# Partial sums of an output product added in DRAM by DMAs that GpSimd issues, instead of on VectorE

## The chip, the cores and the metric

The kernel runs on one core of one Trainium2 chip. The metric is the device time of one execution in microseconds (us); lower is better. TensorE is written PE (its weight loads PEld), VectorE DVE, ScalarE ACT, GpSimd POOL and SyncE SP, as in the profile.

## The reference, cut to what matters

Causal attention over 2 batches of 12 heads (448 positions, 64 wide) gives a matrix x of 896 tokens by 768 features. Two dense stages follow.

```python
a = x @ w1;  b = x @ w2
y = (a * b @ w3) @ w_out                 # first stage, 768 -> 1024 -> 768
h = y @ w_in                             # second stage, 768 -> 2048
g = h * clip(h + 3.0, 0.0, 6.0) / 6.0
out = g @ moe2_w_out                     # 2048 -> 768
```

The last product is the one the change touches. The kernel calls its weights v_out and it works on transposed data: the result is 768 rows (6 blocks of 128) by 896 columns (2 halves of 448).

## The kernel before, in words

Every 32-bit product is made of three passes: each operand is split into a high and a low part, and high*high, high*low and low*high are accumulated in one PSUM bank. A matmul here is 128 by 128 weights against 448 columns. Some products use a seven-product scheme of Strassen's kind (P1 to P7), in which sums and differences of blocks are formed by DVE ahead of time.

The 2048 rows of the last product are cut into NC = 4 parts of 512, c = 0 to 3, so that a part can be multiplied as soon as its piece of g is there. The list `work` gives the order: `pg` units (`gated`, line 943) make g, `po` units (`collected`, line 1049, for c = 0, 1, 2, and `joined`, line 1012, for c = 3) multiply it by v_out. For c = 1, 2, 3 the order is pg, po, pg, po, po, each po belonging to the part before; the three `joined` units come last, each of them with the seven products on banks X, Y and Z.

A `collected(c, i)` unit has four groups of 12 matmuls, for row blocks m = i and i + 3 (j = 0, 1) and halves b = 0, 1. Each group fills one bank, and `evict` (line 772) empties it. The sums of the parts live in DRAM, in `sums_of[m, b]`, 128 by 448 words (224 KB) each. For c = 0, ACT copies the bank to an SBUF tile `o` and SP stores it. For c = 1 and 2, SP first loads the old sum into `o`, DVE adds the bank to it, and SP stores `o` again. `joined` loads the sums of three parts into four tiles `o[m, b]`, adds its seven products to them on DVE and stores to `out`.

The tiles `o` come from tags with two buffers each: `c22` for b = 0, `a2` for b = 1. The tag `a2` also carries a value of `gated`, the tags `a1` and `r` serve `joined(1)`. In the order of the program the last users of `a2` are: `gated(7)`, groups 2 and 4 of `collected(2, 1)`, groups 2 and 4 of `collected(2, 2)`, then `o[0, 1]` and `o[1, 1]` of `joined(0)`. A tile can be filled only when the user two places before it is done with the buffer.

What is issued on each engine, and in what order, is fixed when the kernel is built, by a list scheduler (`Plan.issue`). It goes through the operations in simulated time; each engine takes the ready operation of the lowest rank. Ranks in this part are `DENSE` plus the unit's number; a unit's weights are prepared two units ahead (`ahead`, rank + `AHEAD`). The planner's costs are written in the code: an SP issue 0.6 us and 3.2 us more until the data is there (line 94), a copy of a bank on ACT 0.06 + 448 * 0.00083 us, an addition on DVE 0.065 + 448 * 0.00104 us, a result of PE 0.2 us after its end, others 0.15 us. An operation on POOL counts as landed 0.1 us after its end, and lasts longer by every DVE operation marked `ports` that starts beside it (lines 203 to 212); the splits of weights are so marked. On the chip each engine then runs its list in that order and waits on semaphores.

POOL's own work in this part is splitting weights (line 337, tiles vja, vjb for pg, voa for `joined`).

Of the kernel before, what the change touches and what calls it, by code (L numbers as in the profile page):

```python
# [14 lines left out]
ALU = mybir.AluOpType  # L15
# [19 lines left out]
DENSE = 100.0  # L35
# [182 lines left out]
def attention_moe_moe2(ctx: ExitStack, tc, q, k, v, w1, w2, w3, w_out, v_in, v_out, out):  # L218
# [8 lines left out]
    nc = tc.nc  # L227
    B, H, S, D = SHAPE
# [69 lines left out]
    def act(n, sb=False):  # L298
        return n * 0.00105 if sb else 0.06 + n * 0.00083

    def dve(n):
        return 0.065 + n * 0.00104
# [157 lines left out]
    plan = Plan()  # L460
# [9 lines left out]
    def scratch(tag, name):  # L470
        if tag == "a1":
            return plan.tile(lambda: xp.tile([P, S], F32, tag=tag, name=name, bufs=2), tag, 2)
        return plan.tile(lambda: later["ab"].tile([P, S], F32, tag=tag, name=name, bufs=2), tag, 2, (done2,))
# [232 lines left out]
    for p in range(HK):  # L706
        x, b, b11, b21 = xt[p, 1], bf[p + HK], xt[p, 0], xt[p + HK, 0]
# [21 lines left out]
    def dense_bank(name):  # L729
        return plan.tile(lambda: later["ps"].tile([P, 512], F32, tag="dl", name=name), "psdl", 8 - DENSE_BANKS, (done,))  # L730

    def bank(name):
        i = count["bank"] % 8
        count["bank"] += 1
        if i < DENSE_BANKS:
            return plan.tile(lambda: pd.tile([P, 512], F32, tag="d", name=name), "psd", DENSE_BANKS)
        return dense_bank(name)

    def cols(b):
        return slice(b * S, (b + 1) * S)  # L740

    def halves(t, b):
        return [t.at((b, HI)), t.at((b, LO))]
# [27 lines left out]

    def evict(ps, m, b, n, c, o):
        rank = DENSE + n
        if c:
            plan.op("dve", dve(S), lambda: nc.vector.tensor_tensor(o[:, :], ps[:, :S], o[:, :], ALU.add),  # L775
                    reads=[ps], writes=[o], rank=rank)
        else:
            plan.op("act", act(S), lambda: nc.scalar.copy(o[:, :], ps[:, :S]), reads=[ps], writes=[o], rank=rank)
        plan.op("sp", 0.6, lambda: nc.sync.dma_start(sums_of[m, b], o[:, :]),
                reads=[o], writes=[summed.at((m, b))], rank=rank)  # L780


    ab, open_ = {}, {}
# [35 lines left out]
    def spare(name):  # L819
        return plan.tile(lambda: later["t"].tile([P, S], F32, tag="c22", name=name, bufs=2), "c22", 2, (done,))  # L820
# [61 lines left out]
    n = after_jobs  # L882
# [38 lines left out]
    for p in range(HK):  # L921
        group = [(m, b) for b in range(B) for m in (p, p + HK)]
        ps = {g: bank("px%d_%d" % g) for g in group}
        for kk in range(KF):
            for m, b in group:
                def go(kk=kk, m=m, b=b, n=n + (m != p), ps=ps):
                    for a, c in ((HI, HI), (HI, LO), (LO, HI)):
# [5 lines left out]
                        writes=[ps[m, b]], rank=DENSE + n)  # L933
# [5 lines left out]
    sums_of = dp.tile([KD, B, P, S], F32, name="sums_of")  # L939
    summed = Handle(plan, None, None, 0)  # L940
# [108 lines left out]
    def collected(c, i):  # L1049
        n = first_of["po", c, i]  # L1050
        for j in range(2):
            m = i + HK * j
            for b in range(B):
                name = f"po{c}_{m}_{b}"
                ps = dense_bank(name) if j else plan.tile(
                    lambda name=name: pd.tile([P, 512], F32, tag="d", name=name), "psd", DENSE_BANKS)
                o = scratch("a2", f"o{c}_{m}_{b}") if b else spare(f"o{c}_{m}_{b}")
                if c:
                    plan.op("sp", 0.6, lambda o=o, m=m, b=b: nc.sync.dma_start(o[:, :], sums_of[m, b]),
                            reads=[summed.at((m, b))], writes=[o], rank=DENSE + n - 2)  # L1060
                for kk in range(KC):
                    def go(ps=ps, n=n, at_=((j * 2 + kk % 2) * 2 + kk // 2) * P, k=c * KC + kk, kk=kk, b=b):
                        for a, d in ((HI, HI), (HI, LO), (LO, HI)):
                            nc.tensor.matmul(  # L1064
                                ps[:, :S], hls[n][:, a, at_:at_ + P], gt[k][:, d, cols(b)],
                                start=kk == 0 and a == d, stop=kk == KC - 1 and a == LO)

                    plan.op("pe", 0.6, go, kind="r", reads=[hls[n], *halves(gt[c * KC + kk], b)], writes=[ps], rank=DENSE + n)
                evict(ps, m, b, n, c, o)

    for w in work:
        if w[0] == "pg":
            gated(w[1])
            for i in range(2):
                ahead(first_of[w] + i)
        else:
            joined(w[2]) if w[1] == NC - 1 else collected(*w[1:])
            ahead(first_of[w])
            while pending:
                between(*pending.pop())  # L1080
# [66 lines left out]
```

## Time and profile before

| | us |
|---|---|
| median of 3 runs | 543.11 (542.46 to 543.97) |
| the profiled execution | 543.72 |
| its span, first to last instruction | 541.9 |
| PE busy in the span | 533.7 |
| DVE / ACT / POOL busy | 407.5 / 306.3 / 120.6 |

The profile is of one execution. The span leaves out some 1.8 us around the instructions. The part that the change touches runs from about 405 us (the first `pg` unit after c = 0) to 512 us, and `joined` runs from there to the end.

### The profile page before, as it was taken

What the parts mean: (1) busy time and instruction counts of PE and PEld (TensorE: products, weight loads), DVE (VectorE), ACT (ScalarE), POOL (GpSimd) and SP (SyncE); (2) the same over time, 40 slices, a digit from 0 to 9 for tenths busy, and PEclk for the clock granted to TensorE, in tenths of its full rate; (3) what the DMA queues carried; (4) which work ended last, traced back from release to release, by engine and by line L of the source; (5) the groups of instructions that cost most, each with busy time, mean ns of one, the idle gap of its engine ahead of it and who ended that gap; (6) DMA issues with size and microseconds to landing.
All of it is one profiled execution on the core that took longest, in us unless ns stands there. A gap on an engine that the chain in (4) does not pass through costs nothing.

```text
span 541.9 us, 8054 instructions
## 1 busy us (share of the span) xinstructions
PE 533.7 (98%) x2863; PEld 482.6 (89%) x2863; DVE 407.5 (75%) x778; ACT 306.3 (57%) x597; POOL 120.6 (22%) x156
## 2 busy tenths in 40 slices
PE   8999999999999999999999999999999999999997
PEld 6787887789999999999999998899899999999996
DVE  4998887647914799897728649999947795799664
ACT  4987878877425555544525335978655651666100
POOL 4787874540501111120000111000000000010100
PEclk9999999999999999999999999999999999999999
DMA  8988876214133333322513012628283857372745
GB/s 289 356 291 268 320 245 206 91 62 158 47 114 131 117 116 117 118 97 99 212 60 116 1 59 76 236 97 317 79 285 110 269 183 259 112 252 76 256 152 186
DMA packets 33512, 89.91 MB, mean 166 GB/s; under 512 B 3264, under 2 KB 21952, under 8 KB 30912
## 3 DMA queue, kind: packets, MB, share of 16 engines
q1 hardware_dynamic: 33472, 89.40, 48.4%
q8 instruction: 22, 0.36, 0.3%
q14 instruction: 18, 0.15, 0.1%
HBM read 75.24 MB, written 14.16 MB: 165 GB/s over the span
## 4 chain that ended last, share of the span: by engine, by line
PE 88%; DVE 5%; issue 3%; DMA 1%; ACT 1%; POOL 0%; SPq 0%; POOLq 0%; DVEq 0%
PE po L1064 15%; PE pw L664 12%; PE paX L812 11%; PE px L928 10%; PE pgX L812 8%; PE s L529 7%; PE paZ L812 5%; PE o L595 4%; PE pgZ L812 4%; PE ptp L578 4%; PE paY L812 3%; PE pgY L812 2%; PE poX L812 1%; PE warm L621 1%; DMA ks<-in_k 1%
## 5 line engine op out<-in xcount | busy, mean ns | idle before, releaser
L1064 PE MATMUL po<-g,vo 128*128 128x448 f32 x432 | 87.9, 362 | 0.0
L1064 PEld LDWEIGHTS po<-g,vo 128*128 128x128 f32 x432 | 81.0, 187 | 5.4
L664 PE MATMUL pw<-wr,w 128*128 128x384 f32 x384 | 69.9, 340 | 0.0
L664 PEld LDWEIGHTS pw<-wr,w 128*128 128x128 f32 x384 | 66.4, 188 | 0.5
L555 POOL TENSOR_SCALAR prb<-prb,sums 128x64 f32<-128x64 f32 (+6 forms) x84 | 58.7, 715 | 36.0 <-DVE sums L549 24.5
L928 PE MATMUL px<-ab,wp 128*128 128x448 f32 x288 | 57.8, 362 | 0.0
L928 PEld LDWEIGHTS px<-ab,wp 128*128 128x128 f32 x288 | 54.0, 187 | 3.6
L536 ACT ACTIVATE prb<-prb,sums 128x64 f32<-128x64 f32 (+6 forms) x84 | 42.1, 505 | 12.9 <-DVE sums L532 12.4
L529 PE MATMUL s<-ks,qs 128*128 128x128 f32 (+6 forms) x168 | 46.1, 399 | 1.4 <-DMA ks<-in_k 1.2
L337 POOL TENSOR_SCALAR vja<-vir 128x768 fp32r<-128x768 f32 x8 | 7.7, 957 | 172.2 <-DVE x2t L751 70.1
L532 DVE CUSTOM_DVE_ANT_0 prb<-s,maskb 128x64 f32<-128x64 f32 (+6 forms) x84 | 32.8, 415 | 14.1 <-PE s L529 11.9
L529 PEld LDWEIGHTS s<-ks,qs 128*128 128x128 f32 x168 | 26.9, 195 | 8.0 <-DVE sums L532 2.9
L583 ACT COPY pt<-ptp 128x512 f32<-128x512 f32 x48 | 26.2, 584 | 9.2 <-PE ptp L578 9.1
L578 PE MATMUL ptp<-ident,prb 128*128 128x128 f32 x192 | 27.0, 273 | 0.0
L337 POOL TENSOR_SCALAR w2a<-w1r 128x768 fp32r<-128x768 f32 x8 | 14.4, 1799 | 55.2 <-PE paZ L812 37.2
L578 PEld LDWEIGHTS ptp<-ident,prb 128*128 128x128 f32 x192 | 22.5, 141 | 4.2 <-issue 1.7
L595 PEld LDWEIGHTS o<-pt,vr 128*64 128x64 f32 x192 | 12.7, 136 | 13.0 <-issue 8.7
L595 PE MATMUL o<-pt,vr 128*64 128x448 f32 (+3 forms) x192 | 23.4, 386 | 0.0
L756 ACT ACTIVATE rab<-q,consts 128x448 f32<-128x448 f32 x24 | 16.1, 673 | 12.3 <-DVE q L956 12.3
L775 DVE TENSOR_TENSOR o<-po,o 128x448 f32<-128x448 f32 x24 | 14.9, 620 | 9.9 <-PE po L1064 6.9
L361 ACT ACTIVATE vor<-vor 128x1024 f32<-128x1024 f32 x12 | 13.9, 1161 | 14.5 <-DMA vor<-in_moe_w_out 14.5
L766 ACT ACTIVATE g<-rab 128x448 fp32r<-128x448 f32 x28 | 16.5, 589 | 6.3 <-DVE rab L759 5.6
(181 smaller groups left out, 1157.5 us busy)
## 6 DMA issues: line engine op xcount, KB each, us to landing
vor<-in_moe_w_out SPq DMA_DIRECT2D x12, 1024.0 KB, 5.3
w3r<-in_moe_w SPq DMA_DIRECT2D x8, 1024.0 KB, 7.2
sums_of<-o SPq DMA_DIRECT2D x36, 224.0 KB, 3.2
o<-sums_of SPq DMA_DIRECT2D x36, 224.0 KB, 2.9
wrr<-in_moe_w_out SPq DMA_DIRECT2D x8, 768.0 KB, 7.5
w1r<-in_moe_w SPq DMA_DIRECT2D x8, 768.0 KB, 5.7
w2r<-in_moe_w SPq DMA_DIRECT2D x8, 768.0 KB, 4.3
vjr<-in_moe_w_in SPq DMA_DIRECT2D x8, 768.0 KB, 4.8
```

What stands on the lines that cost most here:

```text
L337: plan.op("pool", single(size), lambda: nc.gpsimd.tensor_scalar(hl[:, HI, at_:at_ + size], x(), 1.0, 1.0, ALU.mult, ALU.mult), reads=reads ...
L529: plan.op("pe", pe4(n), lambda: nc.tensor.matmul(ps[:, :n], qs[u][:, t].rearrange("p h i -> p (h i)"), ks[u][:, :n], start=True, stop=True ...
L532: plan.op("dve", dve(n), lambda: nc.vector.tensor_tensor_reduce(out=z(), in0=ps[:, :n], in1=maskb[:, S - n:], scale=-SCALE, scalar=3.0e38, ...
L536: plan.op("act", 0.29 + n * 0.00083, lambda: nc.scalar.activation(z(), z(), AF.Exp, bias=sm[:, 0, t:t + 1], scale=-1.0, accum_out=sm[:, 1, ...
L555: nc.gpsimd.tensor_scalar(s, s, sm[:, 1, t:t + 1], 1.0, ALU.mult, ALU.mult)
L578: nc.tensor.transpose(ps[:, i * P:(i + 1) * P], pb[:, OFF[t] + kb * P:OFF[t] + (kb + 1) * P], ident)
L583: plan.op("act", act(4 * P), lambda: nc.scalar.copy(d[:, 4 * g:4 * g + 4].rearrange("p n h i -> p (n h i)"), ps[:, :]), reads=[ps], writes ...
L595: nc.tensor.matmul(ps[T * j:T * j + T, kb * P:S], vr[u][:, kb, j, :], d[:, base[kb]:base[kb] + TQ - 2 * kb, j, :], start=kb == 0, stop=kb ...
L664: nc.tensor.matmul(ps[:, :W], weight(n, a, kk), hls[m][:, c, at_:at_ + W], start=kk == 0 and a == c, stop=kk == KF - 1 and a == LO)
L812: nc.tensor.matmul(ps[:, :S], hl[:, a, off + kk * P:off + (kk + 1) * P], t[:, c, at_], start=first and kk == 0 and a == c, stop=kk == n - ...
L928: nc.tensor.matmul(ps[m, b][:, :S], weight(n, a, kk), ab[kk][:, c, cols(b)], start=kk == 0 and a == c, stop=kk == KF - 1 and a == LO)
L1064: nc.tensor.matmul(ps[:, :S], hls[n][:, a, at_:at_ + P], gt[k][:, d, cols(b)], start=kk == 0 and a == d, stop=kk == KC - 1 and a == LO)
```

## The change

For c = 1 and 2, ACT copies the bank to `o` as it does for c = 0, with no load ahead of it. Then POOL issues a DMA that adds `o` to `sums_of[m, b]` in DRAM. The 24 loads by SP (12 per part), the 24 additions on DVE and the 24 stores by SP go; 24 copies on ACT and 24 adding DMAs on POOL's queue come. `joined` is as it was, with its 12 loads of the sums. The planner counts the adding DMA as a POOL operation of 1.0 us.

```diff
     def evict(ps, m, b, n, c, o):
         rank = DENSE + n
+        plan.op("act", act(S), lambda: nc.scalar.copy(o[:, :], ps[:, :S]), reads=[ps], writes=[o], rank=rank)
         if c:
-            plan.op("dve", dve(S), lambda: nc.vector.tensor_tensor(o[:, :], ps[:, :S], o[:, :], ALU.add),
-                    reads=[ps], writes=[o], rank=rank)
+            plan.op("pool", 1.0, lambda: nc.gpsimd.dma_start(sums_of[m, b], o[:, :], accum_op=ALU.add),
+                    reads=[o], writes=[summed.at((m, b))], rank=rank)
         else:
-            plan.op("act", act(S), lambda: nc.scalar.copy(o[:, :], ps[:, :S]), reads=[ps], writes=[o], rank=rank)
-        plan.op("sp", 0.6, lambda: nc.sync.dma_start(sums_of[m, b], o[:, :]),
-                reads=[o], writes=[summed.at((m, b))], rank=rank)
+            plan.op("sp", 0.6, lambda: nc.sync.dma_start(sums_of[m, b], o[:, :]),
+                    reads=[o], writes=[summed.at((m, b))], rank=rank)
@@ collected
                 o = scratch("a2", f"o{c}_{m}_{b}") if b else spare(f"o{c}_{m}_{b}")
-                if c:
-                    plan.op("sp", 0.6, lambda o=o, m=m, b=b: nc.sync.dma_start(o[:, :], sums_of[m, b]),
-                            reads=[summed.at((m, b))], writes=[o], rank=DENSE + n - 2)
                 for kk in range(KC):
```

## Rows read from the trace of the kernel before

**Rows 1.** The page: the span, and busy time of each engine (share, instructions).

```profile
span 541.9 us, 8054 instructions
PE 533.7 (98%) x2863; PEld 482.6 (89%) x2863; DVE 407.5 (75%) x778; ACT 306.3 (57%) x597; POOL 120.6 (22%) x156
```

**Rows 2.** Windows A:B: length, busy us of PE, PEld, DVE, ACT, POOL; clock; DMA.

```profile
361.40:404.40 43.00, 41.86 (x210) 38.75 (x209) 34.83 (x51) 29.35 (x47) 1.94 (x2) 1.00 0.57 196
404.40:458.40 54.00, 54.00 (x272) 50.63 (x271) 41.28 (x63) 27.79 (x42) 3.93 (x4) 1.00 0.64 211
458.40:512.40 54.00, 54.00 (x271) 50.44 (x270) 45.39 (x78) 26.80 (x43) 5.85 (x6) 1.00 0.52 170
```

**Rows 3.** Timeline of PE: start us, us, line, tiles, count, idle before.

```profile
383.23 2.08 PE L812 MATMUL pgX<-T4g,v 128*128 128x448 f32 x9 [1.14 <-DVE q L956]
...
458.35 1.96 PE L812 MATMUL pgX<-x2t,vja 128*128 128x448 f32 x9
...
512.46 1.36 PE L812 MATMUL poX<-g,voa 128*128 128x448 f32 x6
...
514.87 1.42 PE L812 MATMUL poX<-T2o,voc 128*128 128x448 f32 x6
516.12 1.36 PE L812 MATMUL poZ<-T1o,voa 128*128 128x448 f32 x6
517.32 1.36 PE L812 MATMUL poX<-g,voa 128*128 128x448 f32 x6
...
522.12 1.36 PE L812 MATMUL poZ<-T1o,voa 128*128 128x448 f32 x6
523.56 0.88 PE L812 MATMUL poX<-T3o,voa 128*128 128x448 f32 x3
...
536.88 1.36 PE L812 MATMUL poX<-g,voc 128*128 128x448 f32 x6
```

**Rows 4.** The chain that ended last, its end: start us, us, what.

```profile
536.53 1.76 DMA out<-o
538.29 0.61 DVE o L1027
```

**Rows 5.** One line's instructions, L775 and then L778: ns min/median/max, first and last start.

```profile
L775 DVE TENSOR_TENSOR o<-po,o x24: 609/622/626, 420.0 to 514.7; 128x448 f32<-128x448 f32 x24
...
L778 ACT COPY o<-po x12: 512/534/581, 365.7 to 404.6; 128x448 f32<-128x448 f32 x12
```

**Rows 6.** The stores L779, then the loads L1059: issue ns, and issue to landing.

```profile
L779 SPq DMA_DIRECT2D sums_of<-o x36: 319/319/382, 366.3 to 515.3; - x36
...
DMA to landing us min/median/max: 1.9/3.2/7.5
...
L1059 SPq DMA_DIRECT2D o<-sums_of x24: 319/320/481, 403.2 to 510.2; - x24
...
DMA to landing us min/median/max: 2.4/2.7/5.4
```

**Rows 7.** Timeline of SP's queue at the handover to `joined`.

```profile
515.30 0.32 SPq L779 DMA_DIRECT2D sums_of<-o  x1
...
517.75 1.90 SPq L1023 DMA_DIRECT2D o<-sums_of  x3
```

**Rows 8.** Timeline of DVE at the handover.

```profile
513.12 1.10 DVE L343 TENSOR_TENSOR voc<-vor,voc 128x256 fp32r<-128x256 f32 x3 [1.24 <-ACT voc L341]
...
514.66 0.61 DVE L775 TENSOR_TENSOR o<-po,o 128x448 f32<-128x448 f32 x1
...
523.43 1.14 DVE L1027 TENSOR_TENSOR o<-poZ,o 128x448 f32<-128x448 f32 x2
```

**Rows 9.** Timeline of ACT at the handover, with the idle time before.

```profile
512.66 1.06 ACT L341 CAST voc<-vor 128x256 fp32r<-128x256 f32 x3 [9.02 <-PE po L1064]
```

**Rows 10.** Timeline of POOL: splits of weights, with the idle time before them.

```profile
430.46 1.27 POOL L337 TENSOR_SCALAR vja<-vir 128x768 fp32r<-128x768 f32 x1 [21.32 <-DMA sums_of<-o]
...
503.11 2.62 POOL L337 TENSOR_SCALAR voa<-vor 128x512 fp32r<-128x512 f32 x2 [17.20 <-PE po L1064]
```

## The prediction

> **What bounds the kernel now.** I read the page's busy times first: PE is busy in 533.7 of 541.9 us [rows 1]. A gain must therefore come out of PE's idle time or out of what follows PE's end. Next the windows of the part that changes: from 404.4 to 512.4 PE is busy in every microsecond, while DVE works 41.3 and 45.4 of 54 us and ACT 27.8 and 26.8 [rows 2]. So neither DVE, which is relieved, nor the loads and stores of the sums hold anything up there. The timeline of PE says the same: the last idle of some size is 1.14 us at 383 us, ahead of the first changed operation (the first addition starts at 420.0, rows 5) [rows 3]. After 405 us only two small gaps are left, both in `joined`: six matmuls take 1.20 us (516.12 to 517.32), so the start at 514.87 is 0.01 and that at 516.12 0.05 us late, the one at 523.56 is 0.24 late (522.12 + 1.20) and its three matmuls take longer by about 0.1 [rows 3]. That is 0.4 us, 0.5 at most, and it is all that PE can give back. The end behind PE is an out DMA, a DVE addition and the last stores [rows 4]; the change touches none of them.
>
> **The change, part by part.**
>
> Loads, additions and stores that go: 24 additions of 0.62 us are 14.9 us of DVE [rows 5], and 48 SP issues of 0.32 us are 15.4 us of SP with their waits [rows 6]. All lie beside a PE that never stops, so they are worth nothing, but for the 0.5 us in `joined`.
>
> ACT copies that come: 24 by 0.53 us, the time of the same copy at c = 0, are 12.8 us [rows 5]. ACT goes from 27 to some 33 us of each 54 [rows 2]. What covers them is ACT's idle time: in the 9.0 us before 512.66, where the last four banks are emptied, it does nothing at all [rows 9]. If the cover failed, the cost would be like that of the c = 0 stretch, where ACT and DVE both carried more and PE lost 1.14 us in 43 [rows 2]. I take zero; the ceiling goes into the range.
>
> POOL's queue: the adding DMA waits there for the ACT copy of its bank, and behind it stand the splits of weights for the next pg or `joined` unit. Those splits have room. The split at 430.46 is for the pg unit that PE starts at 458.35 [rows 3], and POOL stood idle 17 and 21 us before the two splits shown [rows 10]. POOL is busy 4 to 6 us of 54 [rows 2]; 12 more issues of even 2 us each would leave it half idle. Zero.
>
> Buffers: before, a buffer had to be stored, loaded again and added to; now it has to be copied to and added in DRAM. Groups end every 2.4 us (12 matmuls of 0.2 us, rows 3), the two buffers of a tag alternate, so a buffer is wanted again 9.6 us after the group that filled it. Copy, handover and adding DMA have to take longer than that before ACT waits, and PE not even then, as eight banks are there. For any adding DMA under about 8 us this is zero.
>
> The handover to `joined(0)` is the one place where the new chain is short of time, and the sum is made there. Tile `o[1, 1]` of `joined(0)` uses the buffer of group 4 of `collected(2, 2)`, whose matmuls end at 512.46 [rows 3]. Before, this buffer was added to at 514.66, stored at 515.30 and loaded again at 517.75 [rows 7, 8]; the addition of P5 to it could run only at 523.43, and the planner had put products of `joined(1)` in front of P7, P3 and P4 of `joined(0)` to bridge that (the start at 517.32 is one, rows 3). After: ACT copies at 512.66 (where it now starts the casts behind the same PE end, rows 9), done at 513.2, POOL issues. Call A the time from there until the adding DMA has landed. Then the load takes 2.7 [rows 6], SP and semaphores 0.3, the DVE addition 0.62 [rows 5]: bank Z is free for P3 at 513.2 + A + 3.6 = 516.8 + A.
>
> What the planner believes decides where PE puts P3. It counts the adding DMA as 1.0 + 0.1 us, where it counted 3.8 for a store. With its costs: copy ends 513.1, POOL starts 513.2; the three voc subtractions on DVE, which fall there [rows 8], are marked `ports` and lengthen the POOL operation by 3 * 0.33, so it counts as landed at 515.3; load 3.8, addition 0.53, and handovers: P3 may start at 519.8. PE is then through with P1, P2, P6, P5 and P7 of `joined(0)` at 518.5 and fills in three steps of 0.6 us of `joined(1)`: P3 stands at about 520.3 in PE's queue. On the chip it starts at 516.8 + A. The stall is A - 3.5, if positive. It isn't given back, since PE has work without a gap from there to its end.
>
> A isn't in the trace. Below it is bounded by the fastest store of the same tile, 1.9; above by a store after a load, as if reading the old sum and writing the new one did not overlap, 3.2 + 2.7, and by the planner's 1.0 for the issue: 6.9 [rows 6]. The DMA does what a store does, with a second read, and its issue is made by another engine; it is nearer to the store with one microsecond for each. I take A = 4.6, so a stall of 1.1 us. The ends give a stall of zero and of 3.4.
>
> The Trainium skill has a price: "DMA: Bandwidth & Descriptors", section on the anatomy of one DMA, gives 2.0 us plus bytes over 436 GB/s for a DMA issued by GpSimd, an estimate of 2.5 us for the 229,376 bytes here. No run here shows it yet; by it the stall would be nil and the sum 0.5 us below the time before. Against that, "Collectives: The Full Stack", section on the bandwidth ceiling, says that the adding transfer is slower because it needs two source reads.
>
> The sum: 0.5 us of small gaps goes, 1.1 comes: +0.6 us. The profiled execution of 543.72 would become 544.3; it lies 0.6 above the median of 543.11, so the median becomes 543.7.
>
> **The rivals.**
>
> (a) The adding DMA is slow, A at 5.6 or more. For it: the fetch of the old sum is a round trip of its own, and stores of this tile have landed as late as 7.5 us [rows 6]. The place is P3 of `joined(0)`, waiting for bank Z. Price: A - 3.5 - 0.5, from +1.6 at A = 5.6 (544.7) to +2.9 at A = 6.9 (546.0). Against it: at 512 us the weights are all loaded and the queues short.
>
> (b) POOL's issue itself is slow or waits, some 3 us or more apiece, so that the adding DMAs come late one behind the other and the c = 2 sums, buffers and splits late with them. POOL's splits at 503.11 stretch to 2.62 us for two [rows 10], which shows that POOL can be held up. With groups every 2.4 us the queue would then grow by 0.6 us or more a group over the eight groups of the last two units, 5 us: A = 9, +5, 548.1. Against it: the room on POOL [rows 10].
>
> (c) PE gains all there is: A under 3.5, no stall, both gaps gone: 542.6. More than that isn't there to be had; a gain of 1.6 us would need a shorter order of PE before 405 us, where nothing changes, or a shorter end.
>
> (d) It doesn't do what it says: DVE is relieved but ACT's copies, queued behind long weight conversions, free the banks later, and PE waits as at c = 0. Price up to 1.14 us a stretch [rows 2], for two stretches 2.3: 545.4.
>
> **How the numbers follow.** The likeliest is the sum with A between 3.5 and 5.5: 0.50. Its own range is 542.6 to 544.7. (a) 0.25, (b) 0.07, (c) 0.12, (d) 0.06. The range for 8 in 10 runs from 542.4 (case c with the scatter of the median) to 546.2 (case a at its upper end), and leaves out (b) and a part of the others. A measurement of this kernel can tell about 0.3%, 1.6 us, from no change. Faster by that: 0.04, as the idle time for it isn't there. Slower by that: (a) 0.25, (b) 0.07 and half of (d): 0.35. Within it: 0.61.
>
> **What would show it right or wrong.** In the profile after: DVE's 24 additions on line 775 are gone, ACT has 36 copies where 12 were. PE is without idle from 405 to 512 as before; an idle there speaks for (d) or (b). At 518 to 524 PE should wait once for bank Z of `joined(0)`, released by a DVE addition that itself waited for the load of the sums; the wait should be the adding DMA's issue to landing less 3.5. A landing under 3.5 us with PE free of gaps is (c). POOL's issue rows longer than 2.4 us each are (b). The prediction is wrong if PE's order before 500 us has changed so that new waits stand there, or if the end behind PE's last matmul grows beyond 3.7 us, since I gave both no cost.

## The result and the profile after

The changed kernel takes 547.43 us, the median of 4 runs (546.73 to 548.58), against 543.54 for the kernel before in the same comparison: a ratio of 1.0077, 95% interval 1.0062 to 1.0092. It is slower by 3.4 to 5.0 us. The profiled execution took 547.92 us. The time lies above the predicted range, whose top was 546.2.

The page of the changed kernel, its span and its busy times:

```profile
span 546.1 us, 8047 instructions
...
PE 535.2 (98%) x2863; PEld 484.0 (89%) x2863; DVE 395.9 (72%) x754; ACT 317.5 (58%) x621; POOL 140.1 (26%) x180
```

Beside [rows 1], DVE has 24 instructions fewer and ACT and POOL 24 more each, so the change did what it says. PE has the same 2863 matmuls.

The windows of the changed kernel (stretch: length, busy us of PE, PEld, DVE, ACT, POOL; clock; share of the DMA engines; GB/s), first the two stretches of [rows 2], then the beginning of `joined` cut finer:

```profile
403.70:457.70 54.00, 54.00 (x272) 50.63 (x271) 33.98 (x51) 32.83 (x52) 13.44 (x15) 1.00 0.60 144
457.70:511.80 54.10, 54.10 (x272) 50.52 (x271) 39.48 (x67) 33.04 (x55) 15.06 (x18) 1.00 0.64 132
511.80:517.30 5.50, 5.50 (x29) 4.92 (x27) 2.26 (x5) 1.50 (x4) 0.87 (x1) 1.00 0.95 150
517.30:520.60 3.30, 0.13 (x1) 0.00 (x0) 0.62 (x1) 0.00 (x0) 0.00 (x0) 1.00 0.82 250
520.60:524.70 4.10, 4.04 (x12) 3.61 (x13) 1.91 (x4) 0.00 (x0) 1.27 (x2) 0.58 0.23 61
524.70:527.20 2.50, 2.50 (x15) 2.33 (x14) 2.14 (x4) 0.00 (x0) 0.00 (x0) 1.00 0.25 92
```

In the first two PE is busy throughout, as before, with ACT at 33 us of 54. In the fourth PE stands still. In the fifth it is busy but gets through 12 matmuls at a granted clock of 0.58, where 15 fit into the next 2.5 us at 1.00.

The timeline of PE in the changed kernel, the rows that answer to [rows 3]:

```profile
382.63 2.08 PE L812 MATMUL pgX<-T4g,v 128*128 128x448 f32 x9 [0.64 <-DVE q L956]
...
511.86 1.36 PE L812 MATMUL poX<-g,voa 128*128 128x448 f32 x6
...
516.66 0.76 PE L812 MATMUL poX<-g,voa 128*128 128x448 f32 x3
...
520.66 2.54 PE L812 MATMUL poX<-T3o,voa 128*128 128x448 f32 x6 [3.23 <-DVE o L1027]
523.00 1.32 PE L812 MATMUL poX<-g,voa 128*128 128x448 f32 x3
...
541.03 1.36 PE L812 MATMUL poX<-g,voc 128*128 128x448 f32 x6
```

From its first matmul to the end of the last (its length, below), `joined` took 536.88 + 1.36 - 512.46 = 25.78 us before [rows 3] and takes 541.03 + 1.36 - 511.86 = 30.53 now: 4.75 us more. The three matmuls at 516.66 end at 517.26 (0.2 each), and P7 of `joined(0)` starts at 520.66: 3.4 us without work. The 12 matmuls behind it take 4.1 us instead of 2.4: 1.7 us. The small gaps of before, 0.4, are gone. 3.4 + 1.7 - 0.4 = 4.7, all of it. `joined` begins 0.6 us earlier than before, 0.5 of it from a shorter wait at 383 us, ahead of the first changed operation; in the profiles below that wait is between 0.6 and 1.2 us, whatever the kernel. The end behind PE is the same 3.7 us.

The chain that ended last, around the wait (start us, us, what it was):

```profile
510.64 4.27 DMA sums_of<-o
514.91 0.02 SPq L1023
...
514.96 0.32 SPq L1023
...
515.38 4.48 DMA o<-sums_of
...
519.98 0.64 DVE o L1027
...
520.66 2.54 PE poX L812 x6
```

Read from the end: P7 waits for bank X, which a DVE addition empties; that waits for the load of `o[0, 1]`, issued at 515.38, which takes 4.48 us. The load stands on SP behind the load of `o[1, 0]` (issued 514.96), and this one waits for the adding DMA of group 3 of `collected(2, 2)`, issued by POOL at 510.64 and landed at 514.91. What `o[0, 1]` itself needs is the adding DMA of group 2, older by a group, 2.4 us.

How it came to this order, by the planner's code: it issues the load of `o[0, 1]` only after the first use of the tile ahead of it in its tag. That was a load before the change, issued at 510.2 at the latest [rows 6]; it is ACT's copy of group 4 now, at 512.10 (its row stands further down). The load of `o[1, 0]` was ready for the planner earlier, since it holds the adding DMA of group 3 for done 0.1 us after the POOL operation.

### The profile page after: what moved, and what is told of

It reads as the page before. It is cut to its first block, busy times and chain, and to the rows that moved or that the text cites. A ratio compares the mean times of both kernels' runs of the same rounds, so it can differ in the third digit from the quotient of the medians.

```text
span 546.1 us, 8047 instructions
## 1 busy us (share of the span) xinstructions
PE 535.2 (98%) x2863; PEld 484.0 (89%) x2863; DVE 395.9 (72%) x754; ACT 317.5 (58%) x621; POOL 140.1 (26%) x180
## 3 DMA queue, kind: packets, MB, share of 16 engines
HBM read 69.73 MB, written 14.16 MB: 154 GB/s over the span
## 4 chain that ended last, share of the span: by engine, by line
PE 78%; DVE 9%; issue 4%; DMA 3%; ACT 3%; POOL 1%; SPq 0%; POOLq 0%; ACTq 0%; DVEq 0%
PE pw L664 12%; PE paX L812 11%; PE px L928 10%; PE po L1061 10%; PE s L529 7%; PE paZ L812 5%; PE pgX L812 5%; PE o L595 4%; PE ptp L578 4%; PE paY L812 3%; PE poX L812 2%; PE pgZ L812 2%; PE pgY L812 1%; PE warm L621 1%; PE poZ L812 1%
## 5 line engine op out<-in xcount | busy, mean ns | idle before, releaser
L776 POOL DMA_DIRECT2D sums_of<-o x24 | 21.2, 882 | 70.7 <-ACT o L774 64.2
L774 ACT COPY o<-po 128x448 f32<-128x448 f32 x36 | 19.2, 532 | 30.6 <-PE po L1061 27.9
L670 ACT COPY g<-pw 128x384 f32<-128x384 f32 x16 | 7.6, 474 | 20.7 <-PE pw L664 15.8
```

## The experiments

The questions: is all of the loss at the handover to `joined`; is it the order of two loads on SP, the adding in DRAM, or the issue from POOL; and what does the clock add. x1 to x4 are compared with a median of before of 543.72 us, all others with 543.54. Edits are shown shortened: words in angle brackets stand for code that is left out, and `...` for lines.

**x1_order: SP's order alone.** The load of `o[1, 0]` has to stand behind that of `o[0, 1]`.

```diff
-  plan.op("sp", 0.6, <load o[m, b]>, ..., rank=rank - 2)
+  loaded[m, b] = plan.op("sp", 0.6, <load o[m, b]>, ..., rank=rank - 2,
+                         after=[loaded[0, 1]] if i == 0 and (m, b) == (1, 0) else ())
```

> Only the order of two loads in SP's queue is changed: in joined(0) the load of o[1, 0] stands behind that of o[0, 1] and not ahead of it. PE's order is that of the changed kernel, row for row. Theory (the load of o[0, 1] was held in SP's queue by the load of o[1, 0], which waited for the adding DMA of a later group): the load of o[0, 1] is issued at about 512.5, when the second group's adding DMA has landed, and not at 515.4; the wait of 3.2 us for bank X ahead of P7 goes, and what is left is P3 waiting for o[1, 1], 1 to 2 us. The time is 1 to 2 us over before (ratio 1.002 to 1.004), 2 to 3 us under the changed kernel. Rival (the wait is the latency of the adding DMA itself, in whatever order): PE's wait stays over 3 us and the ratio at 1.007 to 1.008.

545.0 us, ratio 1.0021 (1.0004 to 1.0038); `joined` took 27.35 us. The wait at P7 is gone. What is left stands at P6, and not at P3 where it was expected. The rows of x1_order on PE, SP and DVE:

```profile
516.55 1.48 PE L812 MATMUL poX<-T2o,voc 128*128 128x448 f32 x6 [1.64 <-DVE o L1028]
...
510.39 0.32 SPq L1023 DMA_DIRECT2D o<-sums_of  x1
512.65 0.32 SPq L1023 DMA_DIRECT2D o<-sums_of  x1
...
515.87 0.62 DVE L1028 TENSOR_TENSOR o<-poX,o 128x448 f32<-128x448 f32 x1 [1.90 <-DMA o<-sums_of]
```

The load at 510.39 is that of `o[0, 0]`. It lands only 5.4 us later, at 515.8; x10_order_g1 asks why. The load at 512.65 is that of `o[0, 1]`, 2.7 us earlier than in the changed kernel. So the order on SP made most of the loss, and a slow load makes what is left.

**x2_busy and x7_busy_again: the clock.** The changed kernel with 12 independent matmuls ahead of P7 of `joined(0)`, so that PE works through the wait.

```diff
+  if i == 0:    # 12 matmuls into an unused bank
+      plan.op("pe", 0.0, busy, kind="r", reads=[comb["vo", i]["A11"][0], X], writes=[<bank>], rank=rank)
   multiply(i, "P7", ...)
```

> The changed kernel, and in PE's queue, just ahead of P7 of joined(0), twelve matmuls of 0.2 us into an unused bank that depend on nothing late. Theory (the 3.3 us of idle PE cost more than themselves, because the matmuls after them ran at a granted clock of 0.58): the clock stays at 1.00 from 520 to 525 and the end comes 1.4 to 1.7 us earlier than in the changed kernel, ratio to before 1.004 to 1.005. Rival (those matmuls were slow because of the transfers beside them or of late operands): they are as slow as before and the time is that of the changed kernel or above, 1.007 to 1.010.

547.39 us, ratio 1.0072 (1.0048 to 1.0096). The rows of x2_busy on PE, and the window behind the wait:

```profile
518.69 2.57 PE L1046 MATMUL busy<-g,voa 128*128 128x448 f32 x12
...
522.01 1.48 PE L812 MATMUL poX<-T3o,voa 128*128 128x448 f32 x6 [0.75 <-DVE o L1027]
...
520.60:524.70 4.10, 3.35 (x17) 2.80 (x16) 2.17 (x4) 0.00 (x0) 1.06 (x2) 1.00 0.38 120
```

In the profile it does what was meant: no drop of the clock, and `joined` at 28.86 us is 1.7 us shorter than in the changed kernel's profile. But `joined` begins 1.4 us later in this execution (513.29 us), after longer waits ahead of it, and the medians can't be told apart: neither the theory's time nor the rival's matmuls. x7_busy_again repeats it beside the changed kernel itself, unedited (x8_after_again).

> The kernel with twelve matmuls ahead of P7 once more, beside the changed kernel itself. Its profile had full clock after the wait, but its time wasn't apart from the changed kernel's. If the low clock after the wait costs 1.5 us, its median lies 1 to 2 us below the changed kernel's of the same series; if the cost is made up elsewhere, within 0.5 us.

> The changed kernel once more, beside the others: ratio to before 1.006 to 1.009, the wait ahead of P7 of joined(0) 2.8 to 3.6 us, and a granted clock well under 1 in the 4 us after it.

547.51 us (1.0074, 1.0058 to 1.0090) with the matmuls and 547.45 us (1.0076, 1.0047 to 1.0105) without: no difference. The profile of x7_busy_again, 549.03 us, has `joined` at 28.73 us, again without a drop of the clock in it; 2.0 us of its excess arise in the first 331 us, where the kernels don't differ. The profiled execution of x8_after_again, 545.32 us, came out otherwise than expected and shows why the clock is no fixed part of the loss. Its rows on PE:

```profile
515.88 1.48 PE L812 MATMUL poX<-T2o,voc 128*128 128x448 f32 x6 [1.09 <-DVE o L1027]
...
519.66 1.47 PE L812 MATMUL poX<-T3o,voa 128*128 128x448 f32 x6 [1.10 <-DVE o L1027]
```

The same kernel here waits twice for 1.1 us, the first time where x1_order waits, and its clock stays at 1.00; `joined` takes 28.18 us. How often an execution has the one long wait with the low clock, and how often the two short ones, isn't settled by one profile of each. The mean granted clock of every execution is on record, and it leans one way: in the four of the result it is 0.996 or 0.997, and the two longest of x8_after_again, 549.96 and 550.87 us, have its lowest, 0.994 and 0.993. But it doesn't say where the clock was low: in the profile of x7_busy_again a mean of 0.997 comes from the first 20 us. And in x2_busy, where no execution is under 0.999, the median is the same. What the clock costs in the median stays open.

**x3_swap and x12_before_swap: the handover alone.** The tags are exchanged so that `joined(0)` uses the buffers of `a1` and `r`, which no group of `collected(2, 2)` uses, and `joined(1)`, later, those of `c22` and `a2`.

```diff
-  scratch(("a2", "r")[i % 2], name) if b else scratch("a1", name) if i % 2 else spare(name)
+  scratch(("r", "a2")[i % 2], name) if b else spare(name) if i % 2 else scratch("a1", name)
```

> The changed kernel, but joined(0) and joined(2) take their four tiles from the tags a1 and r, joined(1) from c22 and a2, so that no load for joined(0) has to wait for an adding DMA of the last collected unit. Theory (all of the loss is the handover to joined(0)): PE waits nowhere for more than 0.5 us after 405 us, the time is that of before or up to 0.6 us below, ratio 0.998 to 1.001. Rival (copies on ACT, issues on POOL or the adding DMAs' traffic slow the whole stretch): ratio 1.003 or more, and idle PE between 405 and 512 us.

543.98 us, ratio 1.0007 (0.9989 to 1.0024); `joined` took 25.53 us, and the trace of PE has no wait after 405 us. All 24 adding DMAs are still there. What they cost is the handover, and nothing of size elsewhere in that execution.

> The kernel before, with the tags of joined(0) to joined(2) exchanged (a1 and r for 0 and 2, c22 and a2 for 1). If the exchange by itself is worth something, it shows here: I expect 0.998 to 1.000, at most the 0.5 us of gaps in joined; 24 additions on DVE and their loads as before.

The same exchange in the kernel before gives 543.2 us, 0.9994 (0.9983 to 1.0005). The exchange is worth nothing by itself, so in x3_swap it gives back the loss and doesn't hide it behind a gain.

**x4_plain: the adding.** The DMAs of POOL store without adding; the parts of the earlier sums are left out of the output.

```diff
-  nc.gpsimd.dma_start(sums_of[m, b], o[:, :], accum_op=ALU.add)
+  nc.gpsimd.dma_start(sums_of[m, b], o[:, :])
```

> The 24 DMAs on POOL's queue store and don't add: the sums of the earlier parts are left out. Every engine's order is that of the changed kernel. If the second read in DRAM is what makes the adding DMA land later than a store issued by SP (4.2 us against 3.2), landing falls to about 3.2 us, the wait ahead of P7 by about 1 us, the time by 1 to 1.5 us. If it is the issue on POOL, landing stays at 3.9 to 4.2 us and the time at that of the changed kernel.

543.11 us, ratio 0.9992 (0.9981 to 1.0003); `joined` took 25.71 us without a wait. The whole loss goes, where 1 to 1.5 us had been expected, and a DMA lands after 2.4 us, not 3.2. Copies on ACT, issues by POOL, the planner's order and the buffers are all those of the changed kernel. The page's row of POOL's queue (packets, MB, share of 16 engines over the span) and its row of traffic with HBM (the DRAM), then the issues of POOL and SP from 405 us on (count, KB each, median us to landing), first of the changed kernel:

```profile
q0 software_dynamic: 3456, 5.51, 7.4%
...
HBM read 69.73 MB, written 14.16 MB: 154 GB/s over the span
...
sums_of<-o POOLq DMA_DIRECT2D x24, 224.0 KB, 4.2
o<-sums_of SPq DMA_DIRECT2D x12, 224.0 KB, 3.5
```

then of x4_plain:

```profile
q0 software_dynamic: 1536, 5.51, 2.6%
...
HBM read 69.73 MB, written 14.16 MB: 155 GB/s over the span
...
sums_of<-o POOLq DMA_DIRECT2D x24, 224.0 KB, 2.4
o<-sums_of SPq DMA_DIRECT2D x12, 224.0 KB, 2.7
```

Adding takes 144 packets for each DMA in place of 64, and 0.074 * 546.1 / 24 = 1.68 us of all 16 engines in place of 0.026 * 542.2 / 24 = 0.59. Groups end every 2.4 us, so by an estimate from these numbers the adding DMAs hold 70% of the engines while they last; the share of all transfers in the window up to 517.3 is 0.95, at only 150 GB/s. With the adding, a DMA lands 1.8 us later, and the loads of the sums 0.8 us later in the median. So most of the loss needs both: the order on SP with a DMA that lands after 2.4 us costs nothing here, and the adding DMAs with the order of x1_order cost a quarter.

**x5_onlylast and x6_notlast: which of the 24.** x5_onlylast has the adding DMAs in `collected(2, 2)` alone, that is 4 of 24; x6_notlast has them everywhere but there. The other units load, add on DVE and store as before the change.

```diff
+  def by_dma(c, m):
+      return c == NC - 2 and m % HK == HK - 1          # x6_notlast: not (...)
...
+  if c and not by_dma(c, m):
+      <load the old sum, add on DVE, store, as before>
+  else:
+      <copy on ACT>
-  if c:
+  if c and by_dma(c, m):
       <adding DMA>
```

> Only collected(2, 2), four of the 24 evictions, goes by ACT copy and adding DMA; the other twenty load, add on DVE and store as in the kernel before. Theory (the loss is made at the handover, by the adding DMAs of that unit and SP's order behind them): PE waits 2 to 4 us ahead of P7 of joined(0) as in the changed kernel, ratio to before 1.005 to 1.008. Rival (the loss grows with the number of adding DMAs and ACT copies): a sixth of it, ratio 1.000 to 1.002.

548.97 us, ratio 1.0084 (1.0057 to 1.0111), with the low clock behind the wait. Its row on PE, and the window behind it:

```profile
521.20 2.52 PE L819 MATMUL poX<-T3o,voa 128*128 128x448 f32 x6 [3.05 <-DVE o L1034]
...
521.20:525.30 4.10, 4.10 (x13) 3.66 (x14) 1.98 (x3) 0.00 (x0) 1.27 (x2) 0.58 0.23 60
```

Four DMAs make the whole loss, so it doesn't grow with their number.

> The other way round: twenty evictions go by adding DMA, only the four of collected(2, 2) load, add on DVE and store as before. Theory (handover only): no wait over 0.5 us after 405 us, ratio 0.998 to 1.001. Rival (number of adding DMAs): five sixths of the loss, 1.005 to 1.007.

547.45 us, ratio 1.0070 (1.0057 to 1.0083): the other twenty make a loss of that size as well. This was a miss. The rows of x6_notlast on PE and DVE, then two steps of the chain that ended last:

```profile
519.30 1.47 PE L819 MATMUL poX<-T2o,voc 128*128 128x448 f32 x6 [2.35 <-DVE o L1034]
...
510.65 0.62 DVE L778 TENSOR_TENSOR o<-po,o 128x448 f32<-128x448 f32 x1 [4.84 <-DMA o<-sums_of]
...
511.77 4.00 DMA sums_of<-o
...
515.79 2.71 DMA o<-sums_of
```

Here `collected(2, 2)` has loads again, beside the adding DMAs of the unit ahead. They take 4.4 us in the median and up to 5.6 (2.7 in the kernel before, [rows 6]), and two of them also wait on SP, up to 2.4 us, for an adding DMA. The first addition of the unit waits 4.84 us for its load; its store goes out at 511.77 and lands after 4.00 us, and only then, at 515.79, can `o[0, 0]` be loaded, which is at 510.05 in the changed kernel. `joined` takes 28.24 us, 2.5 more than before; the rest of this execution's 3.8 stands ahead of it. So the number of adding DMAs doesn't decide, but whether transfers that follow them are needed soon. Here slow loads and stores make most of the lateness; that the planner's order has a part in it isn't shown.

**x9_landing and x11_landing55: the planner's belief.** The changed kernel, planned with adding DMAs that land 3.3 and 5.5 us after the POOL operation, not 0.1.

```diff
-  ready[j] = max(ready[j], end + (self.CHAIN.get(e, 0.0) if near else self.LATENCY.get(e, 0.15)))
+  ready[j] = max(ready[j], end + (3.3 if i in self.far and (i, j) not in order else    # x11_landing55: 5.5
+                             self.CHAIN.get(e, 0.0) if near else self.LATENCY.get(e, 0.15)))
...
+  plan.far.add(<the adding DMA>)
```

> The changed kernel, but the planner counts an adding DMA as landed 3.3 us after its POOL operation and not 0.1 us after. SP then loads o[0, 0], o[0, 1], o[1, 0], o[1, 1] in that order and PE has P3 and P4 of joined(0) behind most of joined(1), but P6 and P7 where they were. Theory (PE's and SP's order were fixed for a landing that came too early): no wait for o[0, 1] and o[1, 1]; left is P6 waiting 0 to 1.6 us for o[0, 0], whose load is slow beside the adding DMAs; ratio 1.000 to 1.003. Rival (order doesn't matter, the adding DMAs slow all of joined(0)): 1.005 or more.

> The planner counts 5.5 us from the end of the POOL operation to the landing, which makes up for the slow loads too. PE has four steps of joined(1) ahead of P6 and more ahead of P7. Theory: no wait over 0.4 us after 405 us, ratio 0.998 to 1.001, at 24 adding DMAs as in the changed kernel.

544.65 us (1.0033, 1.0022 to 1.0044) and 544.94 us (1.0019, 1.0005 to 1.0033). With 3.3 us `joined` is back at 25.77 us without a wait, the length of before; with 5.5 us a wait of 0.57 stands late in it, and it takes 26.33 us. Both medians lie a little above what was expected. What else keeps them above before, in these profiles, stands 50 us earlier. The rows of x9_landing on PE and ACT, and the weight load that they wait for:

```profile
462.17 2.08 PE L815 MATMUL pgX<-T2g,v 128*128 128x448 f32 x9 [0.57 <-ACT q L956]
466.44 2.08 PE L815 MATMUL pgX<-T3g,vjb 128*128 128x448 f32 x9 [0.39 <-ACT q L956]
...
460.11 1.18 ACT L363 ACTIVATE vor<-vor 128x1024 f32<-128x1024 f32 x1 [3.90 <-DMA vor<-in_moe_w_out]
461.16 0.53 ACT L776 COPY o<-po 128x448 f32<-128x448 f32 x1
461.58 0.54 ACT L956 COPY q<-pgX 128x448 f32<-128x448 f32 x1
...
vor<-in_moe_w_out SPq DMA_DIRECT2D x1, 1024.0 KB, 8.8
```

The weight load of 1024 KB (the last row, from 440 to 470 us) lands 8.8 us after its issue, its conversion holds ACT, and behind it on ACT stand the new copy of a bank and the copy that PE waits for. The same conversion in the profile of the changed kernel starts at 459.29 and PE doesn't wait. These waits, 0.4 to 1.0 us in sum, are in the profiles of x2, x6, x7, x9, x10 and x11, and in none of the changed kernel, x1, x3, x4, x5 and x8: by these rows they come and go with when the weight load lands.

**x10_order_g1: what slowed the load in x1_order.** The order of x1_order, and groups 2 to 4 of `collected(2, 2)` store without adding; what these groups should have been added to is left out of the output.

```diff
-  plan.op("pool", 1.0, lambda: nc.gpsimd.dma_start(sums_of[m, b], o[:, :], accum_op=ALU.add),
+  adds = c < NC - 2 or m != HK - 1 and m != KD - 1 or (m, b) == (HK - 1, 0)
+  kind = {"accum_op": ALU.add} if adds else {}
+  plan.op("pool", 1.0, lambda: nc.gpsimd.dma_start(sums_of[m, b], o[:, :], **kind),
```

> The kernel with o[0, 1] loaded ahead of o[1, 0], in which P6 waited 1.6 us for a load of o[0, 0] that took 5.4 us. Here three of the four DMAs of collected(2, 2), those of groups 2 to 4, store and don't add (their old sums are left out); the first adds. Theory (the load of o[0, 0] was slow because the adding DMAs beside it keep the DMA engines busy): it takes 2.5 to 3.7 us, the wait ahead of P6 is under 0.4 us, ratio 0.999 to 1.001. Rival (it was late because group 1's own adding DMA landed late): P6 waits 1 us or more, 1.002 to 1.003.

543.56 us, ratio 1.0003 (0.9990 to 1.0015); `joined` took 25.62 us, with no wait at P6, and none of its loads took more than 3.9 us. So the 5.4 us of the load in x1_order came from the adding DMAs beside it.

None of these versions is faster than the kernel before by what can be measured.

## Why the prediction was wrong

**The place and the length of the new chain were right.** The sum was made at the handover to `joined(0)`, and x3_swap shows that the loss is there: without the handover 1.0007 (up to 1.0024) is left of 1.0077. A, from the end of ACT's copy to the landing, was taken as 4.6 us, between 1.9 and 6.9. For group 3 it is 514.91 - (509.70 + 0.54) = 4.67, by the chain above and the copy's row on ACT (the one below it is group 4's):

```profile
509.70 0.54 ACT L774 COPY o<-po 128x448 f32<-128x448 f32 x1 [1.86 <-PE po L1061]
512.10 0.54 ACT L774 COPY o<-po 128x448 f32<-128x448 f32 x1 [1.86 <-PE po L1061]
```

x4_plain shows that it's the adding that makes A this long. That it does so by a second read, the reason given, isn't shown: the page has the same 69.73 MB read from HBM with the adding and without.

**The step that failed: which product is late, and what its load waits behind.** The prediction followed one tile, `o[1, 1]`, to P3, and allowed 0.3 us for SP and semaphores. It never wrote down SP's own list of loads, though the tile's neighbours have the same new chain. The product that stalled is P7, whose bank X is emptied into `o[0, 1]`, the tile of a group that ended 4.8 us earlier than that of `o[1, 1]`. It would have had time, had its load not stood behind that of `o[1, 0]` in SP's queue, where it went out 0.42 us behind it. Two things were missed there: that the load of `o[1, 0]` waits on the chip for its adding DMA (to 514.91), with other loads behind it; and that, the old load of the sums being gone, the planner now lets `o[0, 1]` go out after a later use of its tag. With the order of x1_order, no product waits at P7 or P3.

The wait that was forecast, P3 for bank Z, was there too, but hidden. Had P7 not waited, P3 would have stood at 517.26 + 2.4 = 519.66, and Z was emptied at 520.86 + 0.62 = 521.48 (the second DVE row below): an estimate of 1.9 us, where 1.1 was forecast. PE lost this time at P7 already.

**A term too small: the load.** It was 2.7 us from [rows 6], the median of the loads of `collected`. For the one that counts it is 4.48, so 1.8 us more, and 5.4 in x1_order. The trace of before had shown that 2.7 was short: the longest load in [rows 6] took 5.4 us, and the loads of `joined` itself, line 1023, took 3.2 in the median:

```profile
L1023 SPq DMA_DIRECT2D o<-sums_of x12: 320/396/463, 502.0 to 531.0; - x12
...
DMA to landing us min/median/max: 2.4/3.2/4.3
```

No bound was put on this term, as was done for A. The two rows of DVE in the changed kernel show the wait for it:

```profile
519.98 0.62 DVE L1027 TENSOR_TENSOR o<-poX,o 128x448 f32<-128x448 f32 x1 [4.63 <-DMA o<-sums_of]
520.86 0.62 DVE L1027 TENSOR_TENSOR o<-poZ,o 128x448 f32<-128x448 f32 x1 [0.25 <-DMA o<-sums_of]
```

**A term left out: the clock.** A wait was counted at its length. In the profiled execution 1.7 us came on top, as the granted clock was 0.58 for 4.1 us behind it; in x8_after_again nothing came on top of two waits of 1.1. In the profiled execution it takes the loss past rival (a)'s highest price: the stall alone, 3.4 - 0.5, is the 2.9 us that was named for A = 6.9. That these agree is chance, as A was 4.67.

**What was right at zero.** DVE's additions and SP's loads and stores were worth nothing: x4_plain has all of them removed and has a ratio of 0.9992 with an interval on both sides of 1. Buffers and ACT's copies cost nothing in the profile after: PE is busy throughout from 403.7 to 511.8. Rival (d) is there in some executions, as the waits of 0.4 to 1.0 us behind a late weight load, less than half of the 2.3 that it was given. Rival (b) is out. The changed kernel's issues of POOL (ns min/median/max) and their landing, then those of the loads in `joined`:

```profile
L776 POOL DMA_DIRECT2D sums_of<-o x24: 837/867/1162, 419.8 to 513.0; - x24
...
DMA to landing us min/median/max: 3.7/4.2/8.4
...
L1023 SPq DMA_DIRECT2D o<-sums_of x12: 319/323/423, 500.0 to 530.9; - x12
...
DMA to landing us min/median/max: 2.5/3.5/4.5
```

An issue takes 0.87 us (0.55 in x4_plain), and behind POOL's work of 13 and 15 us in 54 nothing was late. The end behind PE is unchanged, as assumed.

**The price for a plain DMA.** x4_plain shows a plain DMA issued by POOL landing after 2.4 us; with the adding it is 4.2. The Trainium skill, "DMA: Bandwidth & Descriptors", section on the anatomy of one DMA, gives an estimate of 2.5 us for this size. The trace agrees with it for the plain DMA, and for the adding one the price doesn't hold. The Trainium skill, "Collectives: The Full Stack", section on the bandwidth ceiling, puts the cost of a reducing step down to its two source reads and has nearly half the rate for it, a factor of 1.93. The trace agrees that adding costs the DMA engines more, 1.68 us in place of 0.59, which is a factor of 2.9; the second read itself no row here shows.

**The chances.** Slower by over 0.3% had 0.35, and the likeliest case, with a stall of 1.1 us, had 0.50. The cases differed only in A. A case in which the loads beside the one considered are late was missing, and so the range ended at the highest A.

## What to carry to other kernels

Where a store, a load or an addition moves to another queue, write out the list of every queue that later waits for it, in its order, and ask of each entry behind the waiting one who needs it; the product that stalls can be the neighbour of the one that was moved. A planner that counts a transfer as done when its issue is done can put a load in front of others that could have gone, and correcting its belief (x9_landing, 1.0033) or giving the tile more distance (x3_swap, 1.0007) gave back more than half of the loss or, as far as can be measured, all of it. Work taken from an engine that stands beside a full PE was worth nothing here, so such a change can only be as good as its worst handover.

## What was not expected of the hardware

- An adding DMA of 224 KB from SBUF to DRAM took 1.68 us of all 16 DMA engines and 144 packets, a plain one from the same engine 0.59 us and 64. POOL's own instruction took 0.87 us in place of 0.55, a small part of the 1.8 us by which the landing was later.
- Other transfers beside the adding ones were slower than beside plain ones in the same order (x4_plain): the loads of `joined`, 224 KB, 3.5 us in the median in place of 2.7, the weight loads of 1024 KB from 405 us on 6.6 in place of 5.2. In the kernel before, with loads and stores of its own beside them, the medians were 3.2 and 5.0. The longest say less: a weight load took up to 8.8 in x9_landing, but 8.2 before.
- Behind a wait of 3.2 us in the profiled execution, and of 3.05 us in x5_onlylast, the granted clock was 0.58 for the next 4.1 us: between its two levels of 1.2 and 2.4 GHz on the average. Behind one of 2.35 us in x6_notlast, behind two of 1.1 in x8_after_again, and where matmuls filled the wait in x2_busy, it stayed at 1.00.
